# First batch's q and k by halves of the tokens, and a shorter split of the gates, in an attention-plus-FFN kernel

## The chip, the cores and the metric

The kernel runs on one core of one Trainium2 chip. The metric is device time in microseconds (us) of one execution. The core has five engines that run side by side: TensorE (PE in the profile, with its weight loads shown apart as PEld), VectorE (DVE), ScalarE (ACT), GpSimd (POOL) and SyncE (SP). Transfers are issued by SP, ACT and POOL and carried out by 16 DMA engines; in this kernel only those that POOL issues change the type on the way (float32 to bfloat16).

## The reference

There are 8 batches of 8 heads, 576 tokens, head width 64. Causal attention with a forget gate `f`: the running sum of `log f` is added to the scores as `cum[q] - cum[k]`. Its output, 4608 tokens of 512, goes through a gated FFN of width 1536.

```python
scores = scale * np.matmul(q, k.transpose(0, 1, 3, 2))
log_f = np.log(np.clip(f, 0.0001, 1.0))
cum = np.cumsum(log_f, axis=-1)
decay = cum[:, :, :, None] - cum[:, :, None, :]
scores = np.where(causal, -1000000000.0, scores + decay)
attn = softmax(scores)                       # over the keys
x = np.matmul(attn, v)                       # heads side by side: (4608, 512)
g = x @ w_gate
out = (g / (1 + np.exp(-g)) * (x @ w_val)) @ w_out
```

## The kernel before

**A plan ahead of the code.** The kernel first describes all its work as some 2,480 small operations (`op`, each with engine, duration, what it comes after, which buffers it takes) and lets a planner (`Plan.run`) play them on five engines with modelled durations and a modelled DMA. The order in which the planner starts them is the order in which the instructions stand on each engine of the real program. Each engine then runs its own list strictly in order and waits at an instruction whose inputs are not there yet. A table `ORDER` of one key per operation number decides which ready operation an engine takes first. Where the planner leaves TensorE without work in the first microseconds, it writes matmuls on a constant tile `idle` (line 1296), which compute nothing that is used.

**Attention of the first batch (what the change touches).** q and k of batch 0 come as four "quads" (`ld_quad`, line 558): POOL loads the heads of one group g (heads 0, 1, 4, 5 or 2, 3, 6, 7) of q or k, all tokens, 128 partitions of two rows of 576 numbers, as bfloat16 into the tiles `su`. TensorE transposes them (`turn_two`, line 568, 18 transposes of 64x64 for each pair of heads) into a PSUM bank, ACT or DVE copies the bank into `QK` (`straighten_two`; the copies for the first 256 tokens stand apart from those of the rest). Scores are computed for two heads at once (`score2`, heads jj and jj+4) and in four "banks" (`BANKS`): bank 0 needs queries and keys 0 to 255 only, banks 1 to 3 the others. Then ACT takes the exponential (`expo`, line 762), POOL sets the upper triangle to zero (`mask`, line 771), TensorE multiplies by v (`weigh`, line 785), DVE divides (lines 792, 797), TensorE transposes the result (`flip`, line 802) and it is copied into `xT`, the FFN's input.

**The gates of the first batch.** `f` of the first two batches is loaded, clipped (DVE, line 363), its logarithm taken (ACT, line 366) and summed (DVE scan, line 370), in two parts of the tokens: c0 (0 to 255) and c1 (256 to 575). The sum is added to the scores by extra matmuls with bfloat16 rows, so the float32 sum is split into bfloat16 pieces `KG` on different partitions: `hi` (375), `less` (379), `mid` (383), `less` again, `low` (386), five DVE steps for each part. `choose` (lines 395, 397) makes the query rows `QG` of each of the four head pairs for part c1 from the float32 sum, two on ACT and two on DVE; for part c0 one ACT step `up` (390) serves all.

**The other transfers at the start.** POOL issues, after and between the quads: v of batch 0 (`ld_vb`, line 626), the first third of each FFN weight (line 934), the quads of batch 1 (line 558 again, into `xT`) and part of v of batch 1. SP issues `f`, the constant rows (line 493), the gate rows that batch 1 needs (line 407) and v of batch 1.

**The FFN** starts on the first tokens as soon as its first weights are there (line 943, gate and value matmuls; `tanh` on ACT; products on DVE; output lines 1009, 1016, 1022) and its matmuls then fill TensorE between the attention of the later batches up to the end.

The planner's own model of a transfer from POOL's queue, and where the operations of the first batch are declared:

```python
n.done = t + 1.0 + (0.7 if n.ran == "POOL" and 9.0 < t < 20.0 else 0.0)
...
for g in range(2):
    four(g, -20 + 5 * g)
```

## Time and profile before

| | us |
|---|---|
| three runs | 374.83, 374.86, 376.12 (median 374.86) |
| profiled execution | 374.36 |
| its span, first to last instruction | 372.6 |
| outside the span | 1.8 |
| PE busy | 364.1 (98%) |
| DVE, ACT, POOL busy | 256.8, 212.7, 170.6 |

A busy PE in this profile includes the matmuls on the constant tile, and the ends of pipelined matmuls are modelled. The granted TensorE clock is 1.0 in every slice. The page's slices are 9.3 us long; the first holds most of the idle time of TensorE ahead of the tail.

### The profile page before, as it was taken

To read this page: it belongs to the slowest core of one execution; us is meant where nothing else is said; L and a number is where in the kernel's file an instruction comes from. 1 tells how busy PE (TensorE), PEld (TensorE's weight loads), DVE (VectorE), ACT (ScalarE), POOL (GpSimd) and SP (SyncE) were. 2 spreads that over 40 slices of the span, in tenths; PEclk is the share of its full clock that TensorE was granted. 3 is DMA by queue.
4 is the path that set the end of the run, shared out by engine and by line. 5 is a ranking of instruction groups with operands and counts; after the bars stand their busy time and mean duration, and the time that the engine had idled before them with its cause. 6 is when DMAs were issued, how large, how long until landed. Compare 5 with 4: busy or idle time off the path is not lost.

```text
span 372.6 us, 9646 instructions
## 1 busy us (share of the span) xinstructions
PE 364.1 (98%) x3678; PEld 248.3 (67%) x3712; DVE 256.8 (69%) x608; ACT 212.7 (57%) x439; POOL 170.6 (46%) x396
## 2 busy tenths in 40 slices
PE   7999999999999999999999999999999999999996
PEld 5677556555788646875578855587666964584586
DVE  7888884699937699548963779845788246627633
ACT  6999846265664647755666556577774233323321
POOL 8995544435665516784348523576440400040021
PEclk9999999999999999999999999999999999999999
DMA  8999998996869998999889999799430120011012
GB/s 146 190 196 203 203 198 157 211 199 129 150 150 192 218 159 109 166 216 225 180 168 182 162 224 194 128 149 232 88 38 19 58 84 2 1 58 56 0 58 86
DMA packets 125179, 52.04 MB, mean 140 GB/s; under 512 B 111838, under 2 KB 119582, under 8 KB 124366
## 3 DMA queue, kind: packets, MB, share of 16 engines
q1 hardware_dynamic: 108638, 36.15, 49.9%
q0 software_dynamic: 16288, 15.14, 27.3%
q8 instruction: 29, 0.48, 0.5%
q10 hardware_dynamic: 208, 0.14, 0.1%
q14 instruction: 16, 0.13, 0.1%
HBM read 38.56 MB, written 17.07 MB: 149 GB/s over the span
## 4 chain that ended last, share of the span: by engine, by line
PE 71%; issue 0%; ACT 0%; POOL 0%; DVE 0%
PE ps L943 33%; PE ps L1009 17%; PE ps L728 8%; PE ps L950 6%; PE ps L785 5%; PE ps L1022 3%; POOL PTa L771 0%; ACT PTa L762 0%; ACT PT L762 0%; DVE ot L333 0%; PE ps L802 0%
## 5 line engine op out<-in xcount | busy, mean ns | idle before, releaser
L762 ACT ACTIVATE PT<-ps 128x512 bf16<-128x512 f32 (+2 forms) x192 | 90.4, 518 | 21.2 <-PE ps L728 16.4
L943 PE MATMUL ps<-xT,wv 128*128 128x512 bf16 (+1 forms) x386 | 97.8, 370 | 0.8
L943 PE MATMUL ps<-xT,wg 128*128 128x512 bf16 (+1 forms) x384 | 96.9, 370 | 0.8
L967 DVE SCALAR_TENSOR_TENSOR hh<-th,ps 128x512 bf16<-128x512 f32 (+1 forms) x100 | 66.0, 662 | 19.7 <-PE ps L943 16.1
L954 ACT ACTIVATE th<-ps 128x512 f32<-128x512 f32 (+1 forms) x82 | 47.2, 577 | 53.2 <-PE ps L943 45.7
L771 POOL TENSOR_SCALAR_AFFINE_SELECT PT<-PT 128x128 bf16<-128x128 bf16 (+1 forms) x192 | 54.3, 290 | 50.8 <-ACT PT L762 46.1
L728 PE MATMUL ps<-QK 68*128 68x256 bf16 x392 | 64.0, 261 | 0.4 <-ACT PTa L762 0.2
L964 DVE SCALAR_TENSOR_TENSOR th<-th,ps 128x512 f32<-128x512 f32 (+1 forms) x82 | 53.6, 655 | 13.9 <-ACT th L954 13.6
L943 PEld LDWEIGHTS <-wg 128*128 128x128 bf16 x400 | 37.8, 97 | 34.5
L943 PEld LDWEIGHTS <-wv 128*128 128x128 bf16 x400 | 37.2, 97 | 34.7 <-issue 0.3
L771 POOL TENSOR_SCALAR_AFFINE_SELECT PTa<-PTa 128x256 bf16<-128x256 bf16 x64 | 27.2, 431 | 54.9 <-ACT PTa L762 53.1
L1000 DVE TENSOR_TENSOR su<-hh 128x512 bf16<-128x512 bf16 (+1 forms) x126 | 46.6, 404 | 1.0
L1009 PEld LDWEIGHTS <-su 128*128 128x128 bf16 x420 | 40.4, 97 | 5.4
L785 PE MATMUL ps<-VB,PT 128*128 128x65 bf16 x768 | 43.2, 193 | 0.1
L785 PEld LDWEIGHTS <-PT 128*128 128x128 bf16 x768 | 36.3, 97 | 9.3 <-POOL PT L771 1.0
L728 PEld LDWEIGHTS <-QK 68*128 68x128 bf16 x392 | 31.9, 97 | 12.8 <-issue 0.6
L1042 POOL TENSOR_TENSOR ot<-ot 128x256 f32<-128x256 f32 x14 | 10.1, 724 | 63.6 <-ACT ot L1035 63.6
L957 ACT ACTIVATE th<-ps 128x512 f32<-128x512 f32 x30 | 17.9, 596 | 33.1 <-PE ps L943 27.7
L762 ACT ACTIVATE PTa<-ps 128x384 bf16<-128x384 f32 x64 | 31.1, 492 | 9.0 <-PE ps L728 8.4
L797 DVE TENSOR_TENSOR xn<-ps,rc 128x320 bf16<-128x320 f32 (+2 forms) x72 | 32.2, 452 | 2.0
L1009 PE MATMUL ps<-wt,su 128*128 128x256 bf16 x252 | 32.9, 272 | 0.0
L1035 ACT ACTIVATE ot<-ps 128x512 f32<-128x512 f32 x28 | 16.7, 598 | 27.3 <-PE ps L1009 26.0
(99 smaller groups left out, 406.5 us busy)
## 6 DMA issues: line engine op xcount, KB each, us to landing
out_dram<-ot SPq DMA_DIRECT2D x35, 256.0 KB
natv<-in_v_dram SPq DMA_DIRECT2D x25, 256.0 KB
qk_d<-in_k_dram POOLq DMA_DIRECT2D x24, 144.0 KB, 4.5
qk_d<-in_q_dram POOLq DMA_DIRECT2D x24, 144.0 KB, 4.1
wv<-in_moe_w_val_dram POOLq DMA_DIRECT2D x3, 512.0 KB, 13.5
wg<-in_moe_w_gate_dram POOLq DMA_DIRECT2D x3, 512.0 KB, 12.3
wo<-in_moe_w_out_dram POOLq DMA_DIRECT2D x4, 384.0 KB, 16.4
VB<-in_v_dram POOLq DMA_DIRECT2D x7, 128.0 KB, 7.0
```

The lines of the kernel that those rows point to most:

```text
L728: nc.tensor.matmul(s[:, c : c + w], QK[:KR, hqk[p].i, 1, j * S + kt * P : j * S + (kt + 1) * P], QK[:KR, hqk[p].i, 0, j * S + q0 : j * S + ...
L762: nc.scalar.activation(place(h, i)[:, OFFS[i] : OFFS[i] + c], ps(bs)[:, :c], AF.Exp, scale=0.125)
L771: nc.gpsimd.affine_select(out=d, in_=d, pattern=pat, compare_op=ALU.is_ge, fill=0.0, base=0, channel_multiplier=-1,)
L785: nc.tensor.matmul(o[:, lo : lo + D + 1], pt[:, c : c + P], VB[hvb[b].i][:, kt, hb, : D + 1], start=first and n == 0, stop=last and n == l ...
L797: nc.vector.tensor_mul(XN[bx.i][:, qb : qb + nq, j], o, r)
L943: nc.tensor.matmul(ps(bf)[:, a:b], w[:, ko, fc * P : (fc + 1) * P], xT[:, ko, at : at + b - a], start=ko == 0 and a == 0, stop=ko == KD - ...
L950: nc.tensor.matmul(ps(bf)[:, c * P : (c + 1) * P], w[:, ko, (4 * fq + c) * P : (4 * fq + c + 1) * P], xT[:, ko, lo : lo + P], start=c + ko ...
L954: nc.scalar.activation(TH[bt.i][:, :n], ps(bf)[:, :n], AF.Tanh, scale=0.5)
L964: nc.vector.scalar_tensor_tensor(out=t, in0=t, scalar=1.0, in1=ps(bf)[:, :n], op0=ALU.add, op1=ALU.mult)
L967: nc.vector.scalar_tensor_tensor(out=HH[bh.i][:, r, lo : lo + n], in0=TH[bt.i][:, :n], scalar=by, in1=ps(bf)[:, :n], op0=ALU.mult, op1=ALU ...
L1000: E[e].tensor_tensor(out=o, in0=x, in1=y, op=f)
L1009: nc.tensor.matmul(ps(bf)[:, c * HALF : (c + 1) * HALF], left(g)[:, q * P : (q + 1) * P], right[:, g], start=opens and g == 0, stop=g == K ...
```

## The change

**q and k by halves.** The eight pieces are now (q or k) x (tokens 0 to 287 or 288 to 575) x (heads 0 to 3 or 4 to 7), each 128 partitions of one row of 576 numbers (`ld_half`). Seven are issued by POOL with the cast. The eighth (k, first tokens, heads 0 to 3) is issued by SP as float32 into a free part of `ot`, and cast by one more operation (`narrow_half`), which stands on ACT. `turn_two` now transposes 64 partitions (the two head pairs of a group) of one token half; `straighten_two` copies 128x288, one for each head pair, sixteen in all as before. The first token half of q and k serves bank 0 of all eight heads.

**The split of the gates.** Four DVE steps for each part: `hi` writes 8 times the sum, as bfloat16, into `QS` and no longer into `KG`; `less` once; `mid` with two scalars, into `KG`; `low` subtracts `KG`. `choose` reads the bfloat16 row `QS`, and all four of its instructions stand on DVE. `up` is gone. The constants in `ct` and `one` follow (two more small fills); the score matmuls read a column of `one` where they read a column of `ident`.

**A new order.** Planner constants are others (halved lateness of POOL's transfers, shorter weight transfers, somewhat longer DVE steps), the `ORDER` table is new for all operations, and two tables set for some operations the earliest start in the plan (`READY`) and the engine (`ON`).

```diff
-                            n.done = t + 1.0 + (0.7 if n.ran == "POOL" and 9.0 < t < 20.0 else 0.0)
+                            n.done = t + 1.0 + (0.35 if n.ran == "POOL" and 9.0 < t < 20.0 else 0.0)
...
     def hi(e, c):
-        nc.vector.tensor_scalar_mul(KG[:, c], cum[:, c], -8.0)
+        nc.vector.tensor_scalar_mul(QS[c.start > 0], cum[:, c], -8.0)
-    def less(e, n, c):
-        nc.vector.scalar_tensor_tensor(out=r1[:, c], in0=KG[:, c], scalar=ct[:, n : n + 1], in1=r1[:, c] if n else cum[:, c],
-                                       op0=ALU.mult, op1=ALU.add)
+    def less(e, c):
+        nc.vector.scalar_tensor_tensor(out=r1[:, c], in0=QS[c.start > 0], scalar=ct[:, 0:1], in1=cum[:, c], op0=ALU.mult, op1=ALU.add)
     def mid(e, c):
-        nc.vector.tensor_scalar_mul(KG[:, c], r1[:, c], -8.0)
+        nc.vector.tensor_scalar(out=KG[:, c], in0=r1[:, c], scalar1=ct[:, 1:2], scalar2=ct[:, 3:4], op0=ALU.mult, op1=ALU.add)
     def low(e, c):
-        nc.vector.scalar_tensor_tensor(out=KG[:, c], in0=r1[:, c], scalar=ct[:, 2:3], in1=ct[:, 3:4].to_broadcast([P, c.stop - c.start]),
-                                       op0=ALU.mult, op1=ALU.add)
-    def up(e, c):
-        nc.scalar.activation(QS[c.start > 0], cum[:, c], AF.Copy, scale=8.0)
+        nc.vector.scalar_tensor_tensor(out=KG[:, c], in0=r1[:, c], scalar=ct[:, 2:3], in1=KG[:, c], op0=ALU.mult, op1=ALU.subtract)
...
-            nc.vector.tensor_scalar(out=QG[jj][:, c], in0=cum[:, c], scalar1=s1, scalar2=s2, op0=ALU.mult, op1=ALU.add)
+            nc.vector.tensor_scalar(out=QG[jj][:, c], in0=QS[c.start > 0], scalar1=s1, scalar2=s2, op0=ALU.mult, op1=ALU.add)
...
+    HR = QP // 2
+    STAGE = OT[1].rearrange("p a d -> p (a d)")[:, 2 * DM - S :]
+    def ld_half(e, x, n, u, hw):
+        src = srcs["qk"[x]][:H].rearrange("(u j) (n p t) d -> u n j p (t d)", u=2, n=2, p=HR)[u, n]
+        dst = STAGE if hw else QN[0][2 * x + n][:, u]
+        E[e].dma_start(out=dst, in_=src)
+    def narrow_half(e, x, n, u):
+        copy(e, QN[0][2 * x + n][:, u], STAGE)
...
+                    if (x, n, u) == HW_HALF:
+                        a = op(("SP", 0.5), ld_half, x, n, u, True, key=-40, dma=HW_DMA, packet=100, behind=loads[:3], tag="half")
...
-    for g in range(2):
-        four(g, -20 + 5 * g)
+    halves((-20, -10))
...
+HW_HALF, HW_DMA, HW_AT = (1, 0, 0), 0.4, 4.4
...
 ORDER = {
-    0: 1592.32604, 1: 1534.553225, 2: -255.398752, 4: 1637.490402, 5: 1637.489873, 6: 1637.489694, 7: 1627.267217, 8: -26.563854,
+    0: -39.042637, 1: 300.042958, 2: -39.059278, 4: 1505.003606, 5: -39.0409, 6: 1199.001645, 7: 1298.997851, 8: 1506.002278,
...
+ON = {
+    28: "DVE", 29: "DVE", 30: "DVE", 31: "DVE", 57: "DVE", 70: "ACT", 79: "ACT", 80: "ACT", 83: "ACT", 85: "ACT", 88: "ACT", 92: "DVE",
```

What stands in a row on the engines, at three places. First POOL from its first transfer (`su`: q and k of batch 0, `VB`: v, `wv` and `wg`: FFN weights, `xT`: q and k of batch 1, `ident`: the constant for transposes). Before:

```order
L558 DMA su_105<-in_k_dram 128x2x576
L558 DMA su_104<-in_q_dram 128x2x576
masks.py:197 MEMSET ident 128x128
masks.py:199 ISA
masks.py:199 AFFINE_SELECT ident<-ident 128x128
L558 DMA su_107<-in_k_dram 128x2x576
L558 DMA su_106<-in_q_dram 128x2x576
L626 DMA VB_68<-in_v_dram 64x8x64
L626 DMA VB_68<-in_v_dram 128x8x64 x4
L934 DMA wv<-in_moe_w_val_dram 128x4x512
```

And in the changed kernel:

```order
L562 DMA su_107<-in_k_dram 128x1x576
L562 DMA su_106<-in_k_dram 128x1x576
L562 DMA su_104<-in_q_dram 128x1x576 x2
masks.py:197 MEMSET ident 128x128
masks.py:199 ISA
masks.py:199 AFFINE_SELECT ident<-ident 128x128
L562 DMA su_105<-in_q_dram 128x1x576 x2
L616 DMA VB_68<-in_v_dram 128x8x64
L562 DMA su_107<-in_k_dram 128x1x576
L616 DMA VB_68<-in_v_dram 128x8x64
L553 DMA xT<-in_q_dram 128x2x576
```

Four transfers of two rows became seven of one row, and a quad of batch 1 moved ahead of the last blocks of v.

Second, POOL again from its first masks (`PTa`: bank 0 of a head, `PT`: the other banks). Before:

```order
L771 AFFINE_SELECT PTa_71<-PTa_71 128x2x128
L771 AFFINE_SELECT PTa_72<-PTa_72 128x2x128
L934 DMA wg<-in_moe_w_gate_dram 128x4x512
L771 AFFINE_SELECT PTa_73<-PTa_73 128x2x128
L558 DMA xT<-in_k_dram 128x2x576
L626 DMA VB_69<-in_v_dram 128x8x64
L558 DMA xT<-in_q_dram 128x2x576
L771 AFFINE_SELECT PTa_75<-PTa_75 128x2x128
```

In the changed kernel:

```order
L765 AFFINE_SELECT PTa_71<-PTa_71 128x2x128
L765 AFFINE_SELECT PTa_72<-PTa_72 128x2x128
L616 DMA VB_68<-in_v_dram 64x8x64
L616 DMA VB_68<-in_v_dram 128x8x64
L553 DMA xT<-in_k_dram 128x2x576
L765 AFFINE_SELECT PTa_76<-PTa_76 128x2x128
L765 AFFINE_SELECT PTa_73<-PTa_73 128x2x128
L765 AFFINE_SELECT PTa_71<-PTa_71 128x2x128
L765 AFFINE_SELECT PTa_72<-PTa_72 128x2x128
L928 DMA wg<-in_moe_w_gate_dram 128x4x512
L765 AFFINE_SELECT PTa_74<-PTa_74 128x2x128
```

The first gate weight moved behind the masks, and two blocks of v, which stood ahead of all masks, moved among them. Further down (not shown) the second and third pieces of the FFN weights moved behind the masks of the first batch.

Third, DVE from the scan of c0 (128x256) on (`xT` holds the gate rows here, `ot` the gates of the later batches, `QK<-ps` are straighten copies). Before:

```order
L370 SCALAR_TENSOR_TENSOR xT<-xT 128x256
L375 TENSOR_SCALAR xT<-xT 128x256
L379 SCALAR_TENSOR_TENSOR xT<-xT,ct 128x256
L383 TENSOR_SCALAR xT<-xT 128x256
L379 SCALAR_TENSOR_TENSOR xT<-xT,ct 128x256
L386 SCALAR_TENSOR_TENSOR xT<-xT,ct 128x256
L363 TENSOR_SCALAR ot_112<-ot_112 128x216
L333 COPY QK<-ps_122 128x261
L333 COPY QK<-ps_121 128x261
L370 SCALAR_TENSOR_TENSOR xT<-xT 128x320
L375 TENSOR_SCALAR xT<-xT 128x320
L397 TENSOR_SCALAR xT<-xT,ct 128x320
```

In the changed kernel:

```order
L370 SCALAR_TENSOR_TENSOR xT<-xT 128x256
L375 TENSOR_SCALAR xT<-xT 128x256
L379 SCALAR_TENSOR_TENSOR xT<-xT,ct 128x256
L382 TENSOR_SCALAR xT<-xT,ct 128x256
L363 TENSOR_SCALAR ot_112<-ot_112 128x216
L385 SCALAR_TENSOR_TENSOR xT<-xT,ct 128x256
L370 SCALAR_TENSOR_TENSOR xT<-xT 128x320
L375 TENSOR_SCALAR xT<-xT 128x320
L392 TENSOR_SCALAR xT<-xT,ct 128x320
L379 SCALAR_TENSOR_TENSOR xT<-xT,ct 128x320
L382 TENSOR_SCALAR xT<-xT,ct 128x320
L385 SCALAR_TENSOR_TENSOR xT<-xT,ct 128x320
```

Both parts of the split now stand together, ahead of every straighten copy of DVE. On PE (not shown) 23 and not 21 matmuls on the constant tile stand ahead of the first transposes and 30 in place of 43 in all; ahead of the first FFN matmul stand 18 more transposes of batch 1 and 12 fewer of the v products of line 785 than before.

130 lines of the change are left out of this document (63 added, 67 removed), and 148 rows, old and new, of tables (ORDER, READY).

## The prediction

> **What bounds the kernel now.** I read the page's shares first, then the slices, then stages, then the instructions of the first 26 us on each engine in order of time.
>
> ```profile
> PE 364.1 (98%) x3678; PEld 248.3 (67%) x3712; DVE 256.8 (69%) x608; ACT 212.7 (57%) x439; POOL 170.6 (46%) x396
> PE   7999999999999999999999999999999999999996
> ...
> 5.98:15.33 9.35, 8.42 (x223) 6.41 (x224) 8.58 (x20) 8.41 (x25) 9.34 (x15) 1.00 1.72 184
> 15.33:25.16 9.83, 9.63 (x183) 6.78 (x183) 8.28 (x44) 9.83 (x25) 9.38 (x28) 1.00 1.36 208
> 120.00:160.00 40.00, 39.66 (x366) 25.94 (x369) 29.13 (x62) 26.16 (x55) 20.40 (x51) 1.00 0.98 161
> 370.00:372.60 2.60, 0.00 (x0) 0.00 (x0) 0.07 (x1) 0.00 (x0) 0.00 (x0) 0.99 0.33 101
> ...
> L1296 PE MATMUL ps<-idle 128*128 128x256 bf16 x22 | 3.3, 274 | 0.0
> ```
>
> The columns of a stage are its length and then the busy time of PE, PEld, DVE, ACT and POOL. TensorE is full from some 15 us on (39.66 of 40 in the middle of the kernel); the last 2.6 us are the final copy and store. What a new beginning can win lies ahead of that: from 5.98 to 25.16 TensorE sits idle 0.93 + 0.20 us, and 3.3 us of its busy time are the 22 matmuls on the constant tile (the query over 5.9 to 25.16). So 4.4 us is the most that a better beginning can give behind the first transposes. But in the same time two other engines are full as well: POOL is busy 9.34 of 9.35 us and then 9.38 of 9.83, ACT 9.83 of 9.83.
>
> ```profile
> 5.99 0.66 PE L568 MATMUL ps<-ident,su 64*64 64x64 bf16 x36 [1.08 <-DMA su<-in_k_dram]
> 8.75 0.34 PE L746 MATMUL ps<-QK 64*128 64x256 bf16 x4
> 15.33 0.42 PE L746 MATMUL ps<-QK 64*128 64x192 bf16 x4
> 23.88 0.41 PE L596 MATMUL ps<-ident,xT 128*64 128x128 bf16 x8
> 24.34 0.88 PE L785 MATMUL ps<-VB,PT 128*128 128x65 bf16 x24
> 25.16 0.60 PE L943 MATMUL ps<-xT,wg 128*128 128x256 bf16 x4
> 38.86 1.03 PE L943 MATMUL ps<-xT,wg 128*128 128x512 bf16 x3
> ```
>
> First transposes at 5.99, first score at 8.75, first score of banks 1 to 3 at 15.33, first FFN matmul at 25.16. From then on TensorE has work for every gap, so the change is worth what it moves this last point, corrected by what TensorE has or has not done by then. ACT's list up to there (copies of the transposes, exponentials of bank 0, those of banks 1 to 3, the next function table, copies for batch 1):
>
> ```profile
> 12.43 1.28 ACT L331 ACTIVATE QK<-ps 128x261 bf16<-128x261 bf16 x4
> 14.84 1.25 ACT L762 ACTIVATE PTa<-ps 128x384 bf16<-128x384 f32 x3 [0.21 <-PE ps L758]
> 15.98 9.84 ACT L762 ACTIVATE PT<-ps 128x512 bf16<-128x512 f32 x24
> 25.84 1.28 ACT L534 ACT_TABLE_LOAD   x1
> 27.41 1.53 ACT L331 ACTIVATE QK<-ps 64x640 bf16<-64x640 bf16 x2
> ```
>
> **The change part by part.** *The transfers.* The first score needs the first halves of q and k: three halves from POOL and the one from SP; the order puts a half of the second tokens ahead of them, so four halves must come through POOL's queue, as many bytes as the two quads of before, and SP's half (float32, 288 KB) on top.
>
> ```profile
> 3.50:4.00 0.50, 0.50 (x5) 0.36 (x4) 0.50 (x6) 0.03 (x1) 0.50 (x2) 1.00 0.83 111
> 4.00:4.50 0.50, 0.50 (x7) 0.45 (x5) 0.34 (x1) 0.47 (x2) 0.50 (x2) 1.00 1.22 199
> ```
>
> The last number is GB/s. From 4 us on the transfers run at about 200, before that at 111: if SP's half fits the room before 4 us it costs nothing; if all of it collides, 288 KB / 200 GB/s = 1.4 us. I take 0.3, since most of it is issued before 3 us; the first score then comes at about 9.0 instead of 8.75. The cast of the half, 128x576 on ACT, stands between two logarithms and is over before the first transposes are; what it delays is the logarithm of c1, whose scan comes only after 8 us. Both cost nothing here.
>
> *The gates*, on DVE before, and two groups by line:
>
> ```profile
> 7.29 0.49 DVE L386 SCALAR_TENSOR_TENSOR xT<-xT,ct 128x256 bf16<-128x256 f32 x1
> 7.69 0.67 DVE L363 TENSOR_SCALAR ot<-ot 128x216 f32<-128x216 f32 x1
> 8.95 0.87 DVE L370 TENSOR_TENSOR_SCAN xT<-xT 128x320 f32<-128x320 f32 x1
> 13.94 0.55 DVE L386 SCALAR_TENSOR_TENSOR xT<-xT,ct 128x320 bf16<-128x320 f32 x1
> ...
> L363 DVE TENSOR_SCALAR xT<-xT 64x256 f32<-64x256 f32 x1 | 0.2, 239 | 0.0
> L397 DVE TENSOR_SCALAR xT<-xT,ct 128x320 bf16<-128x320 f32 x2 | 1.2, 598 | 0.0
> ```
>
> Low of c0 ends at 7.78, the clip follows, and c1, whose scan starts at 8.95, ends with its low at 14.49. Now one step of about 0.5 (the length of low) is gone ahead of low of c0 and the clip of 0.67 stands there: 7.95. Behind it follow the scan, 0.87, and five steps (hi, choose, less, mid, low) of at most 0.6, the mean of `choose` from float32 (L397): c1 ends by 11.8 at the latest. So banks 1 to 3 no longer wait for the gates.
>
> The first score of banks 1 to 3 then waits for the transposes and copies of k's second half: 9.0, the four pairs of scores of bank 0 and two transposes, which TensorE passes no faster than ACT's copies and exponentials free the banks, some 4.4 us by the ACT rows above (ten copies at 0.28 and four exponentials at 0.38): 13.4 instead of 15.33. These 1.9 us are the gain at this point; 13 constant-tile matmuls at 3.3 / 22 = 0.15 fall away there, 2.0 us.
>
> *What is late next: POOL.* Seven issues stand where four stood, and the masks stand behind them.
>
> ```profile
> 1.33 0.89 POOL L558 DMA_DIRECT2D su<-in_k_dram  x1 [0.82 <-POOLq L1473]
> 2.22 0.74 POOL L558 DMA_DIRECT2D su<-in_q_dram  x1
> 3.49 0.73 POOL L558 DMA_DIRECT2D su<-in_k_dram  x1
> 4.92 4.22 POOL L626 DMA_DIRECT2D VB<-in_v_dram  x5
> 9.08 0.81 POOL L934 DMA_DIRECT2D wv<-in_moe_w_val_dram  x1
> 14.74 1.17 POOL L771 TENSOR_SCALAR_AFFINE_SELECT PTa<-PTa 128x256 bf16<-128x256 bf16 x3
> 17.44 0.90 POOL L626 DMA_DIRECT2D VB<-in_v_dram  x1
> 18.34 1.44 POOL L771 TENSOR_SCALAR_AFFINE_SELECT PT<-PT 128x64 bf16<-128x64 bf16 x6
> ...
> 40.91 0.57 POOL L608 DMA_DIRECT2D qk_d<-in_k_dram  x1
> ```
>
> A half has no row of its own. It lies between the narrowest issue, 0.57 (L608), and the first one, 0.89; I take 0.73, the price of the same load with two rows of 576 in place of one. The changed kernel must pass, from 1.33 to the last mask that TensorE needs ahead of its first FFN matmul: seven halves 0.89 + 6 x 0.73 = 5.3; the constant for transposes (2.96 to 3.49) 0.5; five blocks of v 4.2; three of batch 1, 2.7; four quads of batch 1, 2.9; two weights 1.6; eight masks of bank 0 at 0.39, 3.1; twelve others at 0.24, 2.9. Sum 23.2, end at 24.6. None of them waits by my reckoning (ACT's exponentials, below, are ahead of their masks), so POOL alone sets this. Behind that mask stand three v products (0.1) and a last pair of scores (0.4, as at 15.33), with hand-overs 0.7 us: first FFN matmul at 25.3 (before 25.16), though banks 1 to 3 began 1.9 us earlier. In between TensorE stands about twice, before a v product whose mask is not there, and the planner put no constant-tile matmuls there.
>
> *ACT* gives the bound from the other side, from the first straighten copy on (about 6.8, as before). From start to start in its rows: twelve copies of 288 at 0.28 (four from 12.43 to 13.55), 3.4; eight exponentials of bank 0 at 0.38, 3.0; a fill and a logarithm 0.6; two copies of batch 1's transposes 1.5; 21 exponentials at 0.41 (24 from 15.98 to 25.84), 8.6, to the one that frees the banks of the last score. End at 23.9, first FFN matmul 24.4, if ACT never waits. POOL's 25.3 is later, so POOL decides by this sum.
>
> *What TensorE has done by then.* 18 more transposes of batch 1, at 0.41 / 8 = 0.05, 0.9 us; 12 fewer v products at 0.88 / 24 = 0.037, 0.4 us. Net 0.5 us less remains. `up` gone, two fills more on DVE and two `choose` fewer on ACT lie beside other work and cost nothing: ACT and DVE have room once POOL decides.
>
> *The rest of the order.* From 25 us on all of TensorE's list is rearranged. Before, it idled for 0.34 of 40 us in the stage quoted above, so there is little to win and some tenths to lose: I take 0.1.
>
> Sum: +0.1 (25.3 for 25.16) - 0.5 + 0.1 = -0.3 us. Against the profiled execution, 374.36 (its span of 372.6 and 1.8 around it), that is 374.1; the median of the three runs is 0.5 higher, 374.86, so on their scale it is 374.6. I predict 374.4, between the two, which is no change: under 0.5% (1.9 us) a measurement of this kernel hardly tells from none.
>
> **The rivals.** *A, faster.* A half costs POOL 0.57, as the row at 40.91: six times 0.16 and 0.32 for the first give 1.3 us, POOL ends at 23.3, ACT's 24.4 decides, 0.9 us earlier than my 25.3: 373.5. For it: fewer rows per issue. Against it: the issues at 3.49 and 9.08 cost nearly the same for unlike shapes. It ends below 373.0 only if TensorE also loses nothing of the 4.4 us to ACT.
>
> *B, slower: POOL's chain is held up by DVE.* Two engines seem to get in each other's way: the clip of 216 numbers took 0.67 us while POOL was issuing, the same instruction with 256 numbers 0.24 (both under the gates). The change puts four `choose` on DVE (two before), now from two bytes to two bytes. If each holds POOL for its own length, 0.3 to 0.6 us, POOL's chain grows by 1.2 to 2.4 us and each tenth goes straight into the end: 375.6 to 376.8. It decides from 0.5 us on. Against it: POOL's own issues in the rows above vary by 0.1 only. The Trainium skill ("SBUF — State Buffer", "Who interferes with whom") says that a single-input DVE instruction in its two-port mode and a GpSimd instruction exclude each other for the whole instruction, and that GpSimd cannot write the descriptors of its transfers meanwhile; by that rule B is the case. The 0.67 agrees with that from DVE's side; that POOL waits, no row here shows.
>
> *C, slower: the second third of the weights comes late.* Its first issue moves from 21.48 behind the masks, to about 25.
>
> ```profile
> 21.48 0.77 POOL L934 DMA_DIRECT2D wg<-in_moe_w_gate_dram  x1
> ...
> wg<-in_moe_w_gate_dram POOLq DMA_DIRECT2D x3, 512.0 KB, 12.3
> wv<-in_moe_w_val_dram POOLq DMA_DIRECT2D x3, 512.0 KB, 13.5
> wo<-in_moe_w_out_dram POOLq DMA_DIRECT2D x4, 384.0 KB, 16.4
> ```
>
> Issued at 25.0 and 25.8 and landing 12.3 and 13.5 us later (the last numbers), they are there at 37.3 and 39.3; the first full-width FFN matmuls need them at 38.9 and about 39.8. With the 16.4 of the third row they would be 2 us late: 376.4. Against it: POOL's queue is busy without a break, and as many bytes stand ahead of these as before.
>
> *D, the half on SP brings nothing*, since it shares the DMA engines. Then the first score is at 10.2, and the waits for masks shrink by as much: 374.4 still.
>
> **How the numbers follow.** My case (with D) 0.60, from 373.4 to 375.4; A 0.17, B 0.13, C 0.07, something unseen 0.03. Faster by over 0.5% needs 373.0: half of A and a little of my case, 0.13. Slower needs 376.7: the upper ends of B and C, and the unseen, 0.12. The range from 372.6 to 376.5 takes in all but those ends.
>
> **What would show it.** Right: issues of halves on POOL of 0.7 us; POOL without a gap to 24 us; first score at 8.5 to 9.2; first score with 192 columns at 13 to 14; PE waiting for POOL's masks twice between 16 and 20; 25 us for the first FFN matmul. Wrong: that point below 24 (A, or ACT faster than summed), above 26 (B, with `choose` or POOL's issues lengthened), PE waiting for weights near 39 (C), or idle time of more than 0.5 us after 40.

## The result, and the profile after

The changed kernel takes 384.02 us (median of four runs, 383.43 to 384.33) beside 375.12 before (four runs, 374.83 to 376.12): ratio 1.024, interval 1.0217 to 1.0263. It is slower by 8.9 us; "no change" was forecast, with a range up to 376.5. The profiled execution took 383.78 with a span of 381.9. All medians below are of fast executions; one of run 11 (477.06 us) and one of run 15 (2160.64 us) were slow and are left out.

The page of the changed kernel (shares, slices), then its stages of 5 us, with the columns of the prediction's stages:

```profile
PE 365.8 (96%) x3667; PEld 248.6 (65%) x3699; DVE 256.8 (67%) x610; ACT 212.5 (56%) x437; POOL 172.2 (45%) x399
PE   5589999999999999999999999999999999999997
PEclk9599999999999999999999999999999999999999
```

```profile
5.00:10.00 5.00, 1.14 (x6) 0.46 (x4) 2.08 (x4) 0.00 (x0) 2.76 (x4) 0.96 0.98 150
10.00:15.00 5.00, 0.83 (x28) 0.70 (x30) 0.77 (x3) 1.76 (x4) 1.25 (x2) 0.50 2.05 140
```

The same for the kernel before:

```profile
5.00:10.00 5.00, 3.76 (x115) 3.05 (x117) 4.79 (x11) 4.58 (x14) 5.00 (x7) 1.00 1.26 195
10.00:15.00 5.00, 4.33 (x116) 3.25 (x113) 4.66 (x11) 4.45 (x13) 4.99 (x9) 1.00 2.10 173
```

From 5 to 15 us TensorE, VectorE, ScalarE and GpSimd stand still for much of the time, where before VectorE, ScalarE and GpSimd were nearly full and TensorE was busy for 8.09 of the 10 us. The transfers run at 150 and 140 GB/s instead of 195 and 173, and the granted clock of TensorE falls to a half for 10.24 us, from 9.60 on. The instructions in order of time answer to the prediction's second fence (transposes, first score, first score of banks 1 to 3, first FFN matmul):

```profile
13.18 0.68 ACT L331 ACTIVATE su<-ot 128x576 bf16<-128x576 f32 x1 [8.36 <-DMA ot<-in_k_dram]
13.92 0.26 PE L571 MATMUL ps<-ident,su 64*64 64x64 bf16 x1 [7.78 <-ACT su L331]
14.43 0.99 PE L571 MATMUL ps<-ident,su 64*64 64x64 bf16 x35 [0.25 <-DMA su<-in_k_dram]
17.99 0.50 PE L741 MATMUL ps<-QK 64*128 64x256 bf16 x4
23.18 0.39 PE L741 MATMUL ps<-QK 64*128 64x192 bf16 x4 [0.59 <-DVE QK L333]
34.46 1.05 PE L937 MATMUL ps<-xT,wg 128*128 128x256 bf16 x8
```

First transposes 13.92 (5.99 before), first score 17.99 (8.75), first FFN matmul 34.46 (25.16): 9.3 us late, and the rest takes as long as before (383.78 - 34.46 = 349.3; before 374.36 - 25.16 = 349.2). So the loss lies ahead of that matmul, and the first score is 9.2 us late already: q and k arrive late. The transfers of POOL's queue, before and after (packets, MB, share; then issues with KB each and median us to landing):

```profile
q0 software_dynamic: 16288, 15.14, 27.3%
...
su<-in_k_dram POOLq DMA_DIRECT2D x2, 288.0 KB, 5.2
su<-in_q_dram POOLq DMA_DIRECT2D x2, 288.0 KB, 5.8
```

```profile
q0 software_dynamic: 18896, 15.01, 28.5%
su<-in_q_dram POOLq DMA_DIRECT2D x4, 144.0 KB, 11.6
su<-in_k_dram POOLq DMA_DIRECT2D x3, 144.0 KB, 10.8
```

Half the bytes take twice as long, and there are 2,608 packets more for fewer bytes. By size, the trace has 3,920 packets of 4 bytes on this queue instead of 1,184. The count tells the cause. `ld_half` describes its source as 4 heads x 32 rows x 576 numbers; a head's 32 rows don't join the next head's, so the outermost dimension is 4, while the destination has 128 partitions. The profile does not name the engine of a packet, but the counts come out if each half runs on 4 of the 16 DMA engines, 32 rows on each, and each of the other 12 gets 32 packets of 4 bytes: 12 x 32 = 384, by seven halves 2,688; three more transfers than before bring 16 each, 48. 1,184 + 2,688 + 48 = 3,920. Before, two heads of 64 whole rows joined into one dimension of 128, which by the same count ran on all 16. The Trainium skill ("DMA: Bandwidth & Descriptors", "Why a DMA increments its semaphore by 16 and not by 1") has the rule: a transfer uses the largest number up to 16 that divides the slowest dimension of both sides. The counts here and in the runs below agree with it for 16, 8, 4 and 2. The prediction did not apply it. Runs 1 to 3 change this number alone.

POOL stood as well, since the program has eight completion counters for its loads and the ninth waits for the first (POOL's instructions, changed kernel):

```profile
10.97 0.92 POOL L616 DMA_DIRECT2D VB<-in_v_dram  x1 [3.21 <-DMA su<-in_k_dram]
14.67 0.73 POOL L553 DMA_DIRECT2D xT<-in_q_dram  x1 [2.78 <-DMA su<-in_k_dram]
```

### The profile page after: what moved, and what is told of

It is laid out like the page before. It is cut to its first block, busy times and chain, and to the rows that moved or that the text cites. A ratio compares the mean times of both kernels' runs of the same rounds, so it can differ in the third digit from the quotient of the medians.

```text
span 381.9 us, 9627 instructions
## 1 busy us (share of the span) xinstructions
PE 365.8 (96%) x3667; PEld 248.6 (65%) x3699; DVE 256.8 (67%) x610; ACT 212.5 (56%) x437; POOL 172.2 (45%) x399
## 4 chain that ended last, share of the span: by engine, by line
PE 89%; DVE 3%; DMA 3%; ACT 1%; issue 1%; POOL 0%; POOLq 0%
PE ps L937 41%; PE ps L1003 16%; PE ps L723 9%; PE ps L779 8%; PE ps L944 6%; DMA su<-in_k_dram 3%; PE ps L1016 3%; PE ps L1010 3%; DVE su L994 1%; PE ps L796 1%; PE ps L741 1%; PE ps L586 1%; ACT PTa L756 1%; PE ps L571 0%; DVE QK L333 0%
## 5 line engine op out<-in xcount | busy, mean ns | idle before, releaser
L756 ACT ACTIVATE PT<-ps 128x512 bf16<-128x512 f32 (+2 forms) x192 | 91.4, 513 | 20.6 <-PE ps L723 13.4
## 6 DMA issues: line engine op xcount, KB each, us to landing
wo<-in_moe_w_out_dram POOLq DMA_DIRECT2D x4, 384.0 KB, 13.9
```

Source lines behind the costliest of these rows:

```text
L756: nc.scalar.activation(place(h, i)[:, OFFS[i] : OFFS[i] + c], ps(bs)[:, :c], AF.Exp, scale=0.125)
```

## The experiments

All times are medians, and each ratio is to runs of the kernel before on the same chip (medians of 374.5 to 375.0). In runs 1, 2, 3, 7, 12, 14 and 16 the first batch's q and k rows belong to other heads or tokens than the reference wants; the amount of work stays the same.

**1 to 3. The number of engines alone.** One line of `ld_half` differs; bytes, rows, issues and orders stay.

```diff
-        src = srcs["qk"[x]][:H].rearrange("(u j) (n p t) d -> u n j p (t d)", u=2, n=2, p=HR)[u, n]
+        src = srcs["qk"[x]][:H].rearrange("(u n j) (p t) d -> u n (j p) (t d)", u=2, n=2, p=QP)[u, n]          # e1, 16
+        src = srcs["qk"[x]][:H].rearrange("h (m p t) d -> m h p (t d)", m=4, p=HR // 2)[2 * n + u]             # e2, 8
+        src = srcs["qk"[x]][:H].rearrange("(j u n) (p t) d -> u n j p (t d)", u=2, n=2, p=QP)[u, n]            # e3, 2
```

> The changed kernel with one line changed: each of the eight half loads takes two whole heads (128 rows that follow each other in a regular step) instead of 32 rows of each of four heads. Same bytes, rows of the same 2304 bytes, same issues, queues and order; the first batch's q and k hold the wrong tokens, so its attention is computed from wrong rows. Theory (spread): a load whose source has four heads as its slowest dimension runs on 4 of the 16 DMA engines, 32 rows of 107 ns each, with 384 packets of 4 bytes as filling on the other 12; with 128 rows in one dimension it runs on 16. Then the 4-byte packets fall from 3,920 to about 1,230, the first transposes start near 6 us instead of 13.92, the first FFN matmul stands near 25.5 instead of 34.46, and the time is 374 to 376 us. Rival (collision): SyncE's uncast half delays everything on the shared engines: still 381 or more. Rival (many loads): eight loads in flight with eight completion counters hold GpSimd: still 381 or more.

> As the run with two whole heads, but each half load takes 16 rows of each of eight heads, so the slowest dimension is 8 (wrong tokens again, the same bytes and rows). Theory (spread): 8 engines a load, 16 rows of 107 ns each, and 8 engines x 16 = 128 fillings of 4 bytes for each of seven loads on GpSimd's queue (about 900 more than with two whole heads, so about 2,130). First transposes between 7 and 10 us, time 375.5 to 380 us, between the run with whole heads and the changed kernel. The rivals collision and many loads: as the changed kernel, 382 to 385.

> As before, but each half load takes two heads that do not follow each other, 64 rows each, so the slowest dimension is 2 (wrong tokens, same bytes and rows). Theory (spread): 2 engines a load, 64 rows x 107 ns = 6.8 us each at least, 14 x 64 = 896 fillings for each of seven loads, 6,272 more than with whole heads (about 7,500 in all). The time is above the changed kernel's, 386 to 400 us. The rivals: as the changed kernel, 383 to 385.

Queue and first transposes, 16 engines:

```profile
q0 software_dynamic: 16208, 15.00, 27.4%
...
6.33 0.99 PE L571 MATMUL ps<-ident,su 64*64 64x64 bf16 x36 [0.79 <-ACT su L331]
9.09 0.34 PE L741 MATMUL ps<-QK 64*128 64x256 bf16 x4
```

8 engines:

```profile
q0 software_dynamic: 17104, 15.00, 27.1%
...
9.33 1.21 PE L571 MATMUL ps<-ident,su 64*64 64x64 bf16 x36 [4.07 <-ACT su L331]
```

2 engines:

```profile
q0 software_dynamic: 22480, 15.02, 28.2%
...
17.92 0.99 PE L571 MATMUL ps<-ident,su 64*64 64x64 bf16 x36 [12.56 <-ACT su L331]
```

| engines | 16 | 8 | 4 (the change) | 2 |
|---|---|---|---|---|
| time, us | 376.4 | 379.59 | 384.02 | 388.09 |
| ratio | 1.005 [1.0024, 1.0076] | 1.013 [1.0109, 1.0151] | 1.024 | 1.0358 [1.033, 1.0386] |
| 4-byte packets | 1,232 | 2,128 | 3,920 | 7,504 |

Time follows the number of engines at equal bytes. With 16 engines 1.75 us of the 8.9 stay (each beside its own runs of the kernel before; the interval of run 1 goes from 0.9 to 2.8), so the step from 16 to 4 is worth some 7.1 us. Run 1 was expected at 374 to 376 us with the first FFN matmul near 25.5; that matmul came at 27.60, which run 12 follows up. Runs 2 and 3 came out as expected.

**4. The uncast half on POOL's queue, through the planner.**

```diff
-                        a = op(("SP", 0.5), ld_half, x, n, u, True, key=-40, dma=HW_DMA, packet=100, behind=loads[:3], tag="half")
+                        a = op(("POOL", SW), ld_half, x, n, u, True, key=-40, dma=HW_DMA, packet=100, tag="half")
```

> The changed kernel with the uncast half issued first on GpSimd's queue instead of SyncE's, still uncast and still narrowed by ScalarE, the sources with four heads as in the changed kernel; output as the reference. Theory (spread): all eight loads still run on 4 engines each: 379 to 386 us. Rival (collision): without a load on SyncE's queue the first transposes come back to 6 to 7 us and the time to 375 to 378.

451.81 us, 1.205: the planner laid out the later stages anew (TensorE busy 17.66 of the 40 us from 80 to 120). The first score came at 14.44, but the run tells nothing on the queue. The lesson went into run 5 and, after run 8 had met the same, into all later ones: orders are kept or written out.

**5. The same with every order kept.**

```diff
-        E[e].dma_start(out=dst, in_=src)
+        nc.gpsimd.dma_start(out=dst, in_=src)
```

> The changed kernel with one word changed: the uncast half is issued from GpSimd (third there, behind k's two) instead of SyncE; the rest of every engine's order is the same, sources still with four heads. Theory (spread, by the fullest engine): on SyncE's queue the half always takes the same four engines, which then carry 32 of its rows beside 2 x 32 rows of GpSimd's halves; in turn with GpSimd's other seven every engine carries 2 x 32 rows, 64 x 107 ns = 6.9 us, so the last needed half lands near 10 instead of 14.3 us, the first transposes start at 8 to 10 us, and the time is 379 to 382 us: better than the changed kernel, and still over the kernel before. Collision alone (four engines are no fault, only the second queue is): 374 to 377. No part of it is SyncE's queue: 383 to 385.

384.51 us, 1.0259 [1.0224, 1.0294]; first transposes:

```profile
13.74 0.99 PE L571 MATMUL ps<-ident,su 64*64 64x64 bf16 x36 [7.73 <-ACT su L331]
```

The expectation fell: that SP's half fills the same engines as a half of POOL's is not what makes the loss. With eight halves on one queue it is as large, which was the third case of the expectation.

**6 and 7. The kernel before, its first batch's four quads as eight halves**, on 16 and on 4 engines; nothing else of the change is in them.

```diff
-        nc.gpsimd.dma_start(out=QN[b][2 * g + x], in_=a[g].rearrange("u q x -> q u x"))
...
+        for u in range(2):
+            nc.gpsimd.dma_start(out=QN[0][2 * g + x][:, u], in_=a[g, u])                      # e6
+            nc.gpsimd.dma_start(out=QN[0][2 * g + x][:, u], in_=srcs["qk"[x]][:H].rearrange(  # e7
+                "(u j) (g p t) d -> u g j p (t d)", u=2, g=2, p=QP // 2)[...
```

> The kernel before with each of the first batch's four quad loads issued as two half loads of 128 rows in one dimension (two whole heads each): eight issues on GpSimd instead of four, all on 16 engines, the order else as before; output as the reference. It prices the four more issues and is the partner of the next run. Theory (spread): 374.5 to 376.5. Many loads (eight loads and their counters are what costs): 379 or more.

> The kernel before with its eight half loads as in the run beside it, but each of 32 rows of four heads, so on four engines (wrong tokens in the first batch's q and k). Theory (spread, by the fullest engine): four loads that follow each other fill the 16 engines, two loads to each, 3.4 us a load: k and q of the first group land together near 6.5 to 7.5 us (before: 5.9 and 7.3), the rest near 10.5; 375 to 378 us, at most 2 us over its partner, though all eight loads are on four engines. If a load on four engines is slow whatever stands beside it: 380 to 386.

375.7 us, 1.0022 [1.0008, 1.0035], and 379.71, 1.0122 [1.0096, 1.0149]. Eight issues instead of four cost 0.7 us; 4 engines instead of 16 cost 4.0 more, beyond what was expected. Stages of 1 us, on 16 engines (the last number is GB/s):

```profile
4.00:5.00 1.00, 1.00 (x7) 0.74 (x5) 0.30 (x3) 0.91 (x3) 1.00 (x3) 1.00 1.21 230
5.00:6.00 1.00, 1.00 (x15) 0.53 (x15) 0.97 (x2) 0.97 (x3) 1.00 (x3) 1.00 1.12 160
6.00:7.00 1.00, 1.00 (x39) 0.92 (x34) 0.90 (x4) 0.94 (x4) 1.00 (x2) 1.00 1.21 203
```

and on 4:

```profile
4.00:5.00 1.00, 1.00 (x7) 0.73 (x5) 0.50 (x2) 0.94 (x3) 0.93 (x4) 1.00 0.53 40
5.00:6.00 1.00, 0.49 (x4) 0.15 (x2) 0.93 (x3) 0.97 (x3) 1.00 (x2) 1.00 0.95 58
6.00:7.00 1.00, 0.00 (x0) 0.00 (x0) 0.93 (x3) 0.71 (x3) 1.00 (x3) 1.00 0.56 74
```

What the rows do, counted from the transfer records: rows of POOL's queue in flight (begun and not yet through) on average in each us since the first of them, and when each of the first four loads landed (first to last of its 16 completions, us of the span).

```
us since the first row   0    1    2    3    4    5    6    7     loads 1 to 4 landed
before, 16 (quads)      9.8 18.6 19.1 18.9 18.9 18.6 27.0 38.1    5.38- 5.94  6.81- 7.35  8.31- 9.28  9.76-10.70
run 6, 16 (halves)     12.2 13.1 18.0 18.7 18.0 18.5 19.4 34.2    4.22- 5.00  5.18- 5.71  6.04- 6.85  6.75- 7.57
run 7, 4 (halves)       3.1  6.4 10.5 12.2 13.3 17.4 16.6 16.6    3.78- 7.46  4.29- 9.93  4.78-11.02  8.04-11.68
after, 4 (halves)       4.0  6.3  6.7  7.6 11.4 13.2 11.8 11.8    3.38-10.68  6.03-14.38  6.53-14.65 10.66-14.97
```

A row itself takes as long (median 107 ns in all four). But one half on 4 engines has 3 to 4 rows in flight where one on 16 has 12, and only several loads issued one behind the other bring the number up; by then the first ones, which TensorE waits for, are late. By this reading the early completions (3.78 in run 7) are of engines that had only 4-byte packets. In the changed kernel SP's half is on the way at the same time, and its last row is through 9.1 us after POOL's first begins, which holds up the cast.

**8. A mended source, through the planner.** Row p of head j goes to partition 4p + j: the outermost dimension is 32, so all 16 engines work, and TensorE transposes 128 columns at once.

```diff
-        src = srcs["qk"[x]][:H].rearrange("(u j) (n p t) d -> u n j p (t d)", u=2, n=2, p=HR)[u, n]
+        src = srcs["qk"[x]][:H].rearrange("(u j) (n p t) d -> u n p j (t d)", u=2, n=2, p=HR)[u, n]
...
-                nc.tensor.transpose(t[D * u : D * (u + 1), i * QP : (i + 1) * QP],
-                                    QN[0][2 * x + n][r, u, i * D : (i + 1) * D], ident[r, r])
+                nc.tensor.transpose(t[D * u : D * (u + 1), i * P : (i + 1) * P],
+                                    QN[0][2 * x + n][:, u, (t0 + i) * D : (t0 + i + 1) * D], ident)
```

> The changed kernel mended, output as the reference: each half load puts row p of head j on partition 4p + j instead of 32j + p, so its slowest dimension is the 32 rows and it runs on 16 engines; the transposes take all 128 partitions, 18 of 128 columns in two banks instead of 36 of 64 for each half of k or q, and the copies out of PSUM pick the heads apart. TensorE has 72 transposes fewer, 144 instructions. Theory (spread): first transposes near 6.3 us and 374 to 377 us, as the run with whole heads (376.4). Beside it: that run's TensorE stopped from 13.10 to 14.71 us at its 449th instruction, 1.46 us behind the landing of a 16 KB packet of instructions; the kernel before stopped at the same instruction, 0.29 us. If these stops are the fetch of TensorE's instructions, the same instruction count now stands 144 later in the work, the stop near 13 us is gone and the time is 373 to 375.

449.68 us, 1.1987, by the planner's new order again (stages, columns as above):

```profile
80.00:100.00 20.00, 1.58 (x18) 1.23 (x18) 0.69 (x2) 1.14 (x4) 8.44 (x20) 0.54 1.25 191
```

**9. The mend with the engines' orders written out** as they are in the changed kernel; a straighten copy takes the two inner or the two outer heads.

```diff
-                    for o in sorted(ready[e], key=lambda o: (o.key, o.n)):
+                    for o in [o for o in ready[e] if at[e] < len(SEQ[e]) and o.n == SEQ[e][at[e]]]:
```

> The changed kernel mended a second time: the half loads put row p of head j on partition 4p + j (32 rows as the slowest dimension, 16 engines), transposes over all 128 partitions, copies out of PSUM for the inner and the outer two heads apart, and now every engine takes its steps in exactly the order that the changed kernel has (written out as a list), so that only the loads, the transposes and their copies differ. Output as the reference. The first mending took 449.7 us because the planner, given the new copies, put the later steps of all engines in another order. Theory (spread): 374 to 376.5 us, first transposes near 6.3 us, first score near 9.2, first FFN matmul 25 to 27.5. If TensorE's stop at its 449th instruction is the fetch of its instructions: 144 transposes' instructions fewer, 22 more of constant tiles; no stop over 0.5 us without a releaser between 12 and 16 us. If the changed kernel's order itself costs 70 us with other transposes: 440 or more.

377.0 us, 1.0071 [1.0047, 1.0094], half a us above the expected range: some 6.5 of the 8.9 us are back (2.4 over its own runs of the kernel before), with the same cut of the tokens. Where TensorE still waits:

```profile
16.28 0.39 PE L750 MATMUL ps<-QK 64*128 64x192 bf16 x4 [0.88 <-ACT QK L333]
20.06 0.28 PE L805 MATMUL ps<-ident,xn 128*128 128x128 bf16 x2 [0.64 <-DVE natv L630]
27.57 1.05 PE L946 MATMUL ps<-xT,wg 128*128 128x256 bf16 x8
```

**10. Run 9 with POOL's loads in the order in which TensorE needs them** (numbers are operations; three loads move).

```diff
-        75, 71, 73, 72, 2, 76, 77, 102, 74, 103, 117, 104, 108, ...
+        71, 73, 72, 2, 75, 74, 76, 77, 102, 103, 104, 117, 108, ...
```

> The mended kernel with GpSimd's first loads in the order in which they are needed: k's and q's first token halves, then k's and q's second halves, then three blocks of v, then the second batch's first quad (the mended kernel has a second half of k first, and the blocks of v between). q's first half should land 0.9 us earlier (a half takes 0.7 to 0.9 us of the stream there), so the first score comes at 8.0 to 8.8 instead of 9.1, and v's second block no later. If TensorE's start bounds the end: 0.5 to 1 us faster than the mended kernel. If GpSimd's chain of issues and masks bounds it: the same within 0.4 us.

378.15 us, 1.0087 [1.0073, 1.0101], 1.15 over run 9 by the medians, which neither case expected (the two intervals overlap). The first score came earlier (9.44 for 10.11), though not by 8.8, but TensorE waited longer for the copies before the scores behind it, among them

```profile
14.27 0.34 PE L750 MATMUL ps<-QK 64*128 64x256 bf16 x4 [0.66 <-DVE QK L335]
```

The first FFN matmul came at 28.62 instead of 27.57. An early first score is worth nothing here by itself.

**11. Run 9 with the uncast half on POOL's queue**, the edit of run 5.

> The mended kernel with the uncast half issued from GpSimd, third there, instead of SyncE; all else the same. It prices what the change wanted of SyncE's queue. If the stream of the 16 engines bounds the loads, the half lands no later and one more issue (0.55 to 0.6 us) lies on GpSimd: 0 to 0.6 us slower than the mended kernel. If the second queue brings a part of its own (its packets interleave with GpSimd's): 0.6 to 1.5 us slower.

378.88 us, 1.0101 [1.0082, 1.0121], 1.9 over run 9, and the first transposes wait 2.11 us for the cast:

```profile
7.90 0.69 PE L574 MATMUL ps<-ident,su 128*64 128x128 bf16 x18 [2.11 <-ACT su L333]
```

By the medians, SP's half is worth 1.9 us with 16 engines, more than both cases gave it. But the intervals of runs 9 and 11 overlap, and the one of the five executions at a granted clock of 1.0 took 377.29, 0.3 over run 9; the other four, at 0.995 on average, took 378.53 to 379.27. So the size is open.

**12. Run 1 with wide transposes**: each 18 of 64 columns become 8 of 128 and 2 of 64, so that TensorE has 128 instructions fewer.

```diff
-        for i in range(QT):
...
+        for i in range(QT // 2):
             for u in range(2):
+                nc.tensor.transpose(t[D * u : D * (u + 1), i * P : (i + 1) * P], QN[0][2 * x + n][:, u, i * D : (i + 1) * D], ident)
```

> The run with two whole heads to a half load (376.4 us), with each block of 18 transposes of 64 columns written as eight of 128 columns and two of 64: the same 1,152 columns through TensorE, the same banks, copies and order, but 128 TensorE instructions fewer ahead of the first values product (the first batch's q and k are wrong tokens in both). If that run's stop from 13.10 to 14.71 us and the half clock behind it come of the fetch of TensorE's instructions (it stood at its 449th instruction, as the kernel before did for 0.29 us): no stop over 0.5 us near 13 us, the granted clock 1.00 from 15 to 18.3 us, first FFN matmul near 25.5 instead of 27.6, and 374.0 to 375.5 us. If it stood for data (a block of v, a mask): the stop stays and so does 376 to 377.

In run 1 TensorE stands 1.61 us and waits for nothing that the profile shows, and then has half its clock:

```profile
14.73 0.31 PE L779 MATMUL ps<-VB,PTa 128*128 128x65 bf16 x5 [1.61 <-issue]
...
13.00:14.00 1.00, 0.12 (x1) 0.03 (x2) 1.00 (x4) 0.77 (x3) 1.00 (x3) 1.00 2.02 179
16.00:17.00 1.00, 1.00 (x16) 0.50 (x10) 0.72 (x16) 0.95 (x3) 1.00 (x3) 0.50 1.71 176
```

In run 12 this is gone and the clock stays at 1.00; 375.55 us, 1.0046 [1.0019, 1.0072], with the first FFN matmul at 26.19 and not near 25.5:

```profile
9.90 0.34 PE L743 MATMUL ps<-QK 64*128 64x256 bf16 x4
14.67 0.39 PE L743 MATMUL ps<-QK 64*128 64x192 bf16 x4 [0.22 <-DVE QK L333]
18.86 0.28 PE L798 MATMUL ps<-ident,xn 128*128 128x128 bf16 x2 [0.79 <-DVE natv L625]
26.19 1.05 PE L939 MATMUL ps<-xT,wg 128*128 128x256 bf16 x8
```

The times alone do not tell runs 1 and 12 apart (1.005 and 1.0046, the intervals lie over each other). The profiled executions differ, 376.99 and 375.56, and run 1's own times go with the clock: two executions at a granted clock of 0.999 or more took 375.02 and 375.21, the other eight, at 0.986 to 0.995, 376.02 to 379.42. Two of run 12's eight still took 378.49 and 378.76, one of them at a clock of 1.0; why is open.

**13. The kernel before with the four-step gates alone.**

```diff
-        nc.vector.tensor_scalar_mul(KG[:, c], cum[:, c], -8.0)
+        nc.vector.tensor_scalar_mul(QS[c.start > 0], cum[:, c], -8.0)
...
-        nc.vector.tensor_scalar_mul(KG[:, c], r1[:, c], -8.0)
+        nc.vector.tensor_scalar(out=KG[:, c], in0=r1[:, c], scalar1=ct[:, 1:2], scalar2=ct[:, 3:4], op0=ALU.mult, op1=ALU.add)
...
```

> The kernel before with the changed kernel's gates alone: four steps a part instead of five and the copy on ScalarE, gate rows from the two-byte part, the constants and the one-hot product to match; loads, planner's costs and every engine's order as before; output as the reference. DVE's chain for the second part loses one step of 0.53 us and ScalarE one of 0.40. If the gates of the second part set when the wide scores begin (14.49 us there, first such score 15.33): up to 0.6 us faster, 374.0 to 374.6 where the kernel before has 374.6. If the wide scores stand behind the masks and ScalarE's exponentials anyway: the same within 0.3 us. If the two-byte copies hold GpSimd's issues up: 0.3 to 1 us slower.

374.45 us beside 374.47, 0.9994 [0.9978, 1.001]. The last step of c1's split ends 0.76 us earlier than before, but the first score of banks 1 to 3 did not move forward (15.33 before), nor did the first FFN matmul (25.16):

```profile
13.18 0.55 DVE L385 SCALAR_TENSOR_TENSOR xT<-xT,ct 128x320 bf16<-128x320 f32 x1
15.27 0.38 PE L1294 MATMUL ps<-idle 128*128 128x256 bf16 x2
15.58 0.42 PE L745 MATMUL ps<-QK 64*128 64x192 bf16 x4
25.31 0.60 PE L941 MATMUL ps<-xT,wg 128*128 128x256 bf16 x4
```

All gate steps of c1 and all copies of the transposes have ended by 14.43 there. From 11.34 on TensorE goes through its list in order, 13 matmuls on the constant tile among it, with one stop of 0.36 us for which the profile shows no releaser, and so comes to this score at 15.58.

**14 and 15. One DVE copy behind the products that TensorE waits for** (0.79 in run 12, 0.64 in run 9), in runs 12 and 9.

```diff
-        ... 60, 119, 120, 161, 163, 175, 151, ...
+        ... 60, 119, 161, 163, 175, 120, 151, ...
```

> The run with wide transposes (375.55 us; wrong tokens in the first batch's q and k), with one step moved on DVE: the second of two copies of the second batch's keys (64 x 640, 0.81 us each, 16.44 to 18.06 us there) stands behind the reciprocal and the two scalings that TensorE's next transposes wait for, not ahead of them; all other orders the same. Theory (order): TensorE's stop from 18.10 to 18.90 us, which stands behind these copies, falls to 0.2 us or less, the first FFN matmul comes at 25.4 to 25.7 instead of 26.19, and the time is 374.7 to 375.1 us. If ScalarE's exponentials or GpSimd's masks take the stop's place: 375.3 to 375.7.

> The mended kernel (377.0 us, output as the reference) with the same step moved on DVE. There TensorE stopped 0.88 us for ScalarE's copies before the first wide score and 0.64 us at the place that this mends. Theory (order): 376.3 to 376.7 us. It stays over the kernel before (374.6) in either case; if the stop is taken over by another engine: 376.8 to 377.2.

375.52 us, 1.0054 [1.0029, 1.008], and 377.39, 1.0084 [1.0064, 1.0105]: nothing won. In run 14 the wait for DVE became two waits for ACT, with the first FFN matmul at 26.20:

```profile
18.48 0.27 PE L800 MATMUL ps<-ident,xn 128*128 128x128 bf16 x2 [0.58 <-ACT PT L760]
19.23 0.34 PE L783 MATMUL ps<-VB,PTa 128*128 128x65 bf16 x6 [0.48 <-ACT QK L333]
```

**16 and 17. Two logarithms ahead of the cast of SP's half on ACT**, in runs 12 and 9: does the cast's place hold up ACT's chain?

```diff
-        8, 10, 1, 13, 14, 70, 16, 17, 61, ...
+        8, 10, 1, 13, 14, 16, 17, 70, 61, ...
```

> The kernel with whole heads and wide transposes (first FFN matmul at 26.19, 375.55 us), with one move on ACT: the two logarithms of the gates' second part (0.97 us, 64x320) stand ahead of the cast of SP's half instead of behind it. ACT waited 1.02 us for that half, so they fit the gap; tokens of the first batch stay wrong as there. If ACT's chain carries what is left: first straighten copy at 7.0 to 7.4 instead of 7.82, first FFN matmul 0.4 to 0.8 earlier (25.4 to 25.8), 374.8 to 375.2. If the end of this stage hangs on something else (transposes, masks, DVE's copies): 26.1 to 26.3 again and 375.4 to 375.7.

> The same move in the mended kernel (right tokens, first FFN matmul at 27.57, 377.0 us). Its first copies, too, come behind the logarithms, and TensorE waits 0.33, 0.23 and 0.88 us for ACT's copies. If ACT's chain carries it: first FFN matmul at 26.8 to 27.2 and 376.2 to 376.6. If not: 27.5 to 27.7 and 376.8 to 377.2.

375.47 us, 1.0028 [1.0011, 1.0044], and 376.97, 1.0058 [1.0043, 1.0073]: no gain, the place of the cast is not it. ACT in run 16:

```profile
7.53 1.20 ACT L333 ACTIVATE QK<-ps 128x288 bf16<-128x288 bf16 x3 [0.64 <-PE ps L576]
9.16 1.51 ACT L333 ACTIVATE QK<-ps 128x288 bf16<-128x288 bf16 x4 [0.43 <-PE ps L576]
...
19.34 6.94 ACT L760 ACTIVATE PT<-ps 128x320 bf16<-128x320 f32 x17
26.30 1.28 ACT L531 ACT_TABLE_LOAD   x1
```

Its first copies came 0.29 earlier than in run 12, and then it waited for the transposes of q until 9.16. From there to 26.30 it has no wait that the profile shows: 17.1 us. No version was faster than the kernel before.

## Why the prediction was wrong, step by step

**The transfers: the step that failed.** It took the halves as the same bytes in another cut and priced only SP's half against the total rate (0 to 1.4 us, 0.3 taken). The rate itself fell, since a half works on 4 engines: first score +9.2 us instead of +0.3. In the sum it is the term +0.1, the first FFN matmul at 25.3: it came at 34.46. Run 1 restores 16 engines, and there the step holds: first score at 9.09, forecast 9.0. The "unseen" case with a chance of 0.03 was the true one.

| of the 8.9 us (each version beside its own runs of the kernel before) | shown by |
|---|---|
| some 7.1: four engines instead of 16 | run 1 (+1.75) for the change (+8.9) |
| 1.75, interval 0.9 to 2.8: left with 16 engines | run 1; run 12 has +1.1, interval 0.7 to 2.7 |

How much of the 1.75 is TensorE's stop and the half clock behind it, the times do not settle; in the two profiled executions it is 1.4.

**The cast at no cost** holds as to its place (runs 16 and 17). But the first transposes wait for it (0.79 us in run 1), since it waits for SP's half.

**The gates.** c1 was to end by 11.8; in run 1 its split ended at 11.73. Banks 1 to 3 were to begin at 13.4. They began at 14.98 in run 1, behind TensorE's stop of 1.61 us (without it at some 13.4, an estimate from these two numbers that no run shows), and at 14.67 in run 12, where TensorE waited 0.22 us for a copy. With the gates alone it was 15.58 (run 13). So it was not the gates that this point waited for in the kernel before: the row at 15.33 shows no wait for them, and TensorE came to it through its own list.

**POOL's chain to 24.6.** A half was sized at 0.73, the first at 0.89. In the changed kernel the halves behind the first took 0.67 to 0.69 and the first 0.87, near that size; in run 1 they took 0.54 to 0.58 and 0.71, near rival A's price. That POOL has no gap was wrong: in the changed kernel it waits 3.21 and 2.78 us for loads to land, and with 16 engines for ACT's exponentials (1.04 us ahead of 11.17 in run 12). POOL does not decide.

**ACT's bound of 24.4.** With 16 engines ACT decides, by this reading, with the first FFN matmul at 26.19 in run 12: run 14 took TensorE's wait for DVE away, and waits for ACT took its place. The sum had it begin at 6.8 without a wait; it runs through only from 9.2. In the kernel before, ACT needs the same 17.1 us from its wait that ends at 8.73 to its table load at 25.84, two short waits (0.34 and 0.21) included. So 0.4 us of the 1.1 left in run 12 is ACT's later beginning, by the same reading; why the first FFN matmul stood 0.7 us ahead of the table load before and 0.15 ahead of it in run 16 was not settled.

**TensorE's -0.5 and the rest of the order, 0.1.** Behind the first FFN matmul stand 349.3 us after and 349.2 before: the sum of the two was +0.1 instead of -0.4.

**The rivals.** A: its price of a half is run 1's, but POOL's time was not what decided. B: some DVE steps are long again (0.87 us for `mid` of 256 numbers, 0.45 for 320, run 16; the same `mid` of 256 takes 0.41 in run 13), but POOL's issues of blocks of v beside them grow by 0.07 at most (0.93 to 0.97 us, 0.90 to 0.92 before); its rule played no part that these runs show. C: no wait for weights near 39 us (TensorE busy 4.97 of 5 us or more from 35 to 40 in runs 1 and 12). D: with 4 engines the half on SP brings nothing (384.51 in run 5, 384.02 in the change); with 16, run 11 is slower by 1.9 us without it, with overlapping intervals.

The sign that was to show it wrong, a first FFN matmul above 26, appeared, but it was tied to B.

## What to carry to other kernels

When a load is cut in another way, look at its outermost dimension on both sides, not only at its bytes: loads with an outermost dimension of 128, 8, 4 and 2, which by the packets ran on 16, 8, 4 and 2 engines, gave 376.4, 379.6, 384.0 and 388.1 us with the same bytes. Its marks in a profile are many more packets of 4 bytes on a queue that should carry rows (3,920 instead of 1,184), and GB/s far under that of the same stage before. To test one line of a kernel whose order is planned, write the order out first: the same edits took 451.81 and 449.68 us through the planner, and 384.51 and 377.0 with the order kept (runs 4, 5, 8 and 9).

## What was not expected of the hardware

**Packets of 4 bytes on idle engines.** The counts fit this rule: each half that POOL loads with the cast on k engines puts as many 4-byte packets on each of the others as it has rows on each of its own (384 for a half on 4 engines). In the changed kernel a packet of 4 bytes takes 9 ns (median). A half on 2 engines so costs 896 of them (run 3: 7,504 in all).

**TensorE's instruction stream.** The profile has a queue for it:

```profile
q8 instruction: 29, 0.48, 0.5%
```

A packet has 16 KB. In run 1 (1.61 us), in run 13 (0.36) and before (0.29) TensorE stops with no releaser at the same place of its list, 447 weight loads and matmuls by the records from its start (the expectations count it as the 449th instruction); in run 1 and before it goes on 1.5 us after the first such packet has landed, in run 13 1.7 us. In run 12, with 128 instructions fewer, it does not stop. That the fetch is the cause is a reading of these coincidences.

**The clock.** It fell to a half at 15.0 us in run 1, 1.9 us after the 1.61 us stop began, and stayed there for 3.41 us; in run 7 for 6.83 us and in the changed kernel for 10.24 us, which are 2 and 3 times that. The Trainium skill ("TensorE: Matmul & The Clock Gate", "Why this matters for your kernels") asks for no idle gaps over about 3 us; here a gap of half that was enough, with TensorE busy for only 0.39 us from 13 to 15.

Where TensorE waits for data anyway, the half clock costs nothing that the times show: of the changed kernel's four executions one had a granted clock of 1.0 and took 384.26 us, the others, at 0.982 to 0.987, 383.43 to 384.33; in run 7 it was 380.52 at 1.0 and 379.41 to 379.84 at 0.990 to 0.991.
